# Gate exponentials in PSUM, 32-bit zero products at the start, and a new order table, in a windowed-attention and adapter-mixture kernel

## The chip, the cores and the metric

The kernel runs on one core of a Trainium2 chip. The metric is the device time of one execution in microseconds (us). The kernel before was timed three times: 145.18, 145.84 and 146.81 us, median 145.84. One further execution was taken by the hardware profiler, and every row shown here is from that one.

## The reference

Eight batches of eight heads attend over 576 positions with a window of 32 to each side; the heads of a batch are laid side by side into rows of 512, and each of the 4608 rows goes through a mixture of eight low-rank adapters (rank 16) of which the two with the highest gate logits are used.

```
scores = scale * (q @ k.T);  scores = where(|i - j| <= 32, scores, -1e9)
attn   = softmax(scores);    x = (attn @ v) as (4608, 512)
logits = x @ w_gate;         the two largest, w = softmax over these two
out    = x + sum over the two experts of w * ((x @ A[e]) @ B[e])
```

## The kernel before, in words

*Names.* TensorE (PE) multiplies, VectorE (DVE) and ScalarE (ACT) move results out of PSUM, GpSimd (POOL) casts inputs and issues the loads of v, SyncE (SP) issues the other loads and all stores. PSUM has eight banks, and the program hands them out as buffers of one or two ("B").

*Loads.* q, k and v are each cut into nine tiles (t = 0 to 8). A tile of q or k is one load on SP's queue (L287) into one of five buffers `raw`; two casts (L296 on ACT, L298 on POOL or DVE) turn its halves into 16 bits (`c16`, six buffers); eight transposes on PE for each half (L306) and an eviction (L316) make `qT` and `kT`. A tile of v comes in four loads on POOL's queue (L328), which write 16 bits, and is turned on DVE (L337).

*Attention.* 36 score tiles: two mask products (L392) and 16 to 20 score products (L397) into two PSUM banks, one exponential on ACT (L404) into `PT`. The products with v (L434, 26 matmuls for a head's five row groups) go to two banks `po`; DVE takes the reciprocal of the row sums (L446) and scales (L459) into `xs`.

*Adapters.* Four sets of rows (s = 0 to 3); the first three are handled ten row groups at a time, the last in parts of 4, 4 and 2, so there are six passes. A pass transposes `xs` (L487), multiplies with `A` and the gate weights at once (L523, forty matmuls in the first three passes) into buffers `pz` of two banks, and then runs the gate on DVE: maximum and difference (L534, L535), the exponential on ACT (L542, `gexp`), then `gate2` (L548 to L555), in which L553 compares the exponentials with the second largest, L554 multiplies the result with them and L555 multiplies with the reciprocal of the sum. `gated` (L565) multiplies the adapter's inner values in PSUM with the gates and frees the `pz` banks. Then transposes (L574), an eviction (`zT`), the second product (L602, with L605 adding x on PE in all but the first set), the copy or sum into `ob` (L613, L616) and the store (L623).

*Order.* The program makes a list of operations, each with its engine or engines, its buffers and its needs. The table `ORDER` gives the order in which they are issued, `ON` the engine where there is a choice, and `HOME` the number of the buffer. Each engine then runs its own instructions strictly in that order, with waits for data and for free buffers. An argument `need` between operations without shared data only restricts the table; it puts no wait into the program. At the start 16 matmuls of zeros (`zw`, L220) run on PE before the first data is there.

## Time and profile before

| | us |
|---|---|
| median of three runs | 145.84 (145.18 to 146.81) |
| the profiled execution's own time | 144.93 |
| its span, first to last instruction | 143.2 |
| busy in the span: PE / DVE / ACT / POOL | 113.8 / 95.8 / 85.9 / 51.3 |
[...]

The span is 1.73 us shorter than the execution's time. A busy PE in the profile is not PE at its peak, since matmuls overlap and their ends are modelled. [...] "Idle before" in a row is the time for which the engine stood still in front of that instruction, with the instruction that ended it.

### The profile page before, as it was taken

The numbers are of one execution on the slowest core, as the hardware profiler recorded it, in microseconds if no ns is written. First come the engines' busy times: TensorE is split into PE (matmuls) and PEld (weight loads), VectorE is DVE, ScalarE is ACT, GpSimd is POOL, SyncE is SP. The second block draws the span as 40 slices with busy tenths as digits, with TensorE's granted clock in tenths as the row PEclk, the third lists the DMA queues.
The fourth block names the chain that finished last, engine by engine and source line by source line (L and its number), as shares of the span: only waits on it lengthen the run. The fifth ranks groups of instructions, "written<-read, shape, count | busy, mean of one in ns | idle before, by whom it ended". The sixth has DMA issues, their size and how long they took to land.

```text
span 143.2 us, 5190 instructions
## 1 busy us (share of the span) xinstructions
PE 113.8 (80%) x2246; PEld 84.5 (59%) x2246; DVE 95.8 (67%) x180; ACT 85.9 (60%) x124; POOL 51.3 (36%) x86
## 2 busy tenths in 40 slices
PE   5934769949797986396999808999899999699840
PEld 2324457747694875275878707667689667577410
DVE  2206536895297869955997895687699688748710
ACT  7214196738775958053886820777639676478770
POOL 6983069459435869404308693000000000000000
PEclk9998777999999999959999985799999999999999
DMA  4999999999999999997487997037000523317885
GB/s 124 361 286 266 301 413 363 338 322 378 334 299 410 323 404 356 285 298 307 79 317 150 292 248 150 0 143 280 13 0 5 183 61 131 123 65 292 281 315 181
DMA packets 13223, 33.90 MB, mean 237 GB/s; under 512 B 2704, under 2 KB 2704, under 8 KB 13200
## 3 DMA queue, kind: packets, MB, share of 16 engines
q1 hardware_dynamic: 11472, 28.86, 55.4%
q0 software_dynamic: 1728, 4.72, 18.0%
q8 instruction: 17, 0.28, 0.8%
q14 instruction: 6, 0.05, 0.1%
HBM read 28.85 MB, written 9.44 MB: 267 GB/s over the span
## 4 chain that ended last, share of the span: by engine, by line
PE 64%; DVE 13%; DMA 11%; issue 5%; ACT 2%; SPq 1%; DVEq 0%; ACTq 0%
PE banks L397 13%; DMA raw<-in_q_dram 11%; PE banks L434 11%; PE banks L306 8%; PE banks L392 7%; PE banks L487 6%; PE banks L602 6%; PE banks L523 6%; PE banks L605 4%; DVE sm L553 3%; DVE sm L555 2%; PE banks L574 2%; DVE xs L459 2%; DVE sm L554 2%; DVE zs L565 1%
## 5 line engine op out<-in xcount | busy, mean ns | idle before, releaser
L404 ACT ACTIVATE PT<-banks 128x1024 f16<-128x1024 f32 x36 | 36.2, 1023 | 15.2 <-PE banks L397 11.8
L298 POOL CAST c<-raw 128x1024 f16<-128x1024 f32 x29 | 29.8, 1045 | 27.9 <-DMA raw<-in_k_dram 12.4
L459 DVE TENSOR_TENSOR xs<-banks,rc 128x640 f16<-128x640 f32 (+1 forms) x33 | 26.4, 802 | 2.3 <-PE banks L487 1.3
L306 PE MATMUL banks<-ident,c 128*128 128x128 f16 x288 | 20.6, 230 | 8.6 <-DVE c L298 4.4
L434 PE MATMUL banks<-vt,PT 64*128 64x65 f16 x832 | 18.9, 194 | 7.2 <-DVE zs L565 3.6
L397 PEld LDWEIGHTS <-kT 64*64 64x64 f16 x608 | 18.8, 114 | 9.9 <-issue 9.8
L397 PE MATMUL banks<-qT,kT 64*64 64x128 f16 (+3 forms) x608 | 24.2, 225 | 0.1
L306 PEld LDWEIGHTS <-c 128*128 128x128 f16 x288 | 18.0, 103 | 10.1 <-DVE c L298 4.5
L434 PEld LDWEIGHTS <-PT 64*128 64x128 f16 x832 | 15.2, 96 | 10.5 <-issue 8.7
L328 POOL DMA_DIRECT2D v<-in_v_dram x36 | 17.9, 502 | 7.3 <-DVE vt L337 5.9
L337 DVE STREAM_TRANSPOSE vt<-v 128x1024 f32<-128x1024 f32 x9 | 18.7, 2072 | 0.6 <-DMA v<-in_v_dram 0.6
L392 PE MATMUL banks<-mask,twice 64*128 64x512 f16 x72 | 15.4, 419 | 4.5 <-DVE zs L565 4.2
L613 ACT COPY ob<-banks 128x1024 f32<-128x1024 f32 (+1 forms) x15 | 13.8, 934 | 3.5 <-PE banks L605 3.0
L602 PE MATMUL banks<-Bw,zT 128*128 128x512 f16 x40 | 14.6, 386 | 1.0 <-DVE zT L177 1.0
L446 DVE RECIPROCAL rc<-banks 128x10 f32<-128x10 f32 (+1 forms) x33 | 7.1, 215 | 12.3 <-PE banks L434 9.1
L179 ACT COPY xT<-banks 128x512 f32<-128x512 f32 x16 | 8.9, 592 | 6.2 <-PE banks L487 6.1
L605 PE MATMUL banks<-xs,ident 128*128 128x512 f16 x30 | 11.6, 386 | 0.0
L487 PE MATMUL banks<-ident,xs 128*128 128x128 f16 x160 | 10.8, 220 | 0.9 <-DVE xs L459 0.9
L487 PEld LDWEIGHTS <-xs 128*128 128x128 f16 x160 | 9.7, 115 | 2.1 <-DVE xs L459 1.0
L523 PE MATMUL banks<-WA,xT 128*128 128x136 f16 x160 | 10.8, 223 | 0.2 <-issue 0.2
L316 ACT COPY kT<-banks 128x512 f32<-128x512 f32 x15 | 8.5, 596 | 4.0 <-PE banks L306 4.0
L316 ACT COPY qT<-banks 128x512 f32<-128x512 f32 x13 | 7.5, 595 | 5.5 <-PE banks L306 5.5
(49 smaller groups left out, 102.9 us busy)
## 6 DMA issues: line engine op xcount, KB each, us to landing
raw<-in_k_dram SPq DMA_DIRECT2D x9, 1024.0 KB, 15.6
raw<-in_q_dram SPq DMA_DIRECT2D x9, 1024.0 KB, 14.7
out_dram<-ob SPq DMA_DIRECT2D x24, 256.0 KB, 2.8
v<-in_v_dram POOLq DMA_DIRECT2D x36, 128.0 KB, 6.8
out_dram<-ob SPq DMA_DIRECT2D x16, 192.0 KB, 2.6
ob<-in_moe_A_dram SPq DMA_DIRECT2D x1, 256.0 KB, 19.5
ob<-in_moe_B_dram SPq DMA_DIRECT2D x1, 256.0 KB, 19.6
wgf<-in_moe_w_gate_dram SPq DMA_DIRECT2D x1, 16.0 KB, 8.1
```

The source lines that it names most:

```text
L298: (nc.vector if eng == "DVE" else nc.gpsimd).tensor_copy(out=o, in_=i)
L306: nc.tensor.matmul(out=ap16(tp)[:, 128 * r:128 * r + 128], lhsT=ap(c16)[:, r], rhs=ident, is_transpose=True, start=True, stop=True)
L328: op("POOL", 0.62, lambda p0=p0, f=f, g=g: nc.gpsimd.dma_start(out=ap(v16)[p0:p0 + 32], in_=src[32 * t:32 * t + 32, f, g]), bufs=[v16], ne ...
L337: nc.vector.transpose(out=o, in_=i)
L392: nc.tensor.matmul(out=p[:, 4 * j:4 * j + 4], lhsT=twice[m], rhs=bcast(mask[m], 1, 4), start=True, stop=False)
L397: nc.tensor.matmul(out=p[m, i, c0:c0 + w], lhsT=ap(kT[t])[m, 64 * s:64 * s + 64], rhs=ap(qT[tq])[m, c:c + w], start=False, stop=(n == len( ...
L404: op("ACT", act(1024), lambda: nc.scalar.activation(out=ap(pt)[:, :, 64:192].rearrange("m i (x b r) -> m i x b r", b=2, r=16), in_=ap(ps). ...
L434: nc.tensor.matmul(out=ap(po)[:, 512 * g + VD * j:512 * g + VD * j + VD], lhsT=ap(PT[ti])[m, pos, off:off + 128], rhs=ap(vt[t])[m, sl, 0:V ...
L459: nc.vector.tensor_tensor(out=o, in0=i, in1=ap(rc)[:, 0:n].to_broadcast([128, n, 2, D]), op=ALU.mult)
L487: nc.tensor.matmul(out=ap16(tp)[:, 512 * i + 128 * c:512 * i + 128 * c + 128], lhsT=ap(xs[s])[:, b, g].rearrange("p (m c) -> p c m", c=4)[ ...
L523: nc.tensor.matmul(out=ap(pz)[:, o:o + ER + E], lhsT=ap(xT)[:, i, c, :], rhs=WA[:, c, :], start=(c == 0), stop=(c == 3))
L602: nc.tensor.matmul(out=o, lhsT=ap(zT)[:, j + i], rhs=Bw, start=True, stop=not by_pe)
```

## The change

Four things are changed at once.

1. The exponentials `e` of the gate are no longer kept in SBUF beside the differences `d` but in PSUM, in 80 unused columns behind the results in the first `pz` buffer. So every operation of `gate2` that has two tensors reads at most one from SBUF. L554 and L555 are also changed round: first `e * sv`, written back to PSUM, then that product times the mask.
2. The zeros of the first products are 32 bits instead of 16, and there are 4 products instead of 16.
3. The rule that the first tile of v is issued after the first load of k in the table (`V_AFTER`) is gone.
4. The tables `ORDER`, `ON` and `HOME` are found anew.

```
-    zw = sb.tile([128, 128], F16, name="zw")
+    zw = sb.tile([128, 128], F32, name="zw")
...
-                    bufs=[v16], need=[(V_AFTER, 0, "raw")] if t == 0 else [],
+                    bufs=[v16],
...
         def pieces():
             a = ap(sm)
-            small = [a[:, 10 * i:10 * i + n] for i in range(3)]
-            wide = [a[:, 40 + 80 * i:40 + 80 * i + E * n].rearrange("p (g e) -> p g e", e=E)
-                    for i in range(3)]
-            return small + wide
+            small = [a[:, 10 * i:10 * i + n].rearrange("p (w g) -> p w g", w=nw) for i in range(3)]
+            wide = [a[:, 40 + 80 * i:40 + 80 * i + E * n].rearrange("p (w g e) -> p w g e", w=nw, e=E)
+                    for i in range(2)]
+            e = ap(pzs[0])[:, 4 * GS + ER + E:4 * GS + ER + E + E * n].rearrange(
+                "p (w g e) -> p w g e", w=nw, e=E)
+            return small + wide + [e]
...
-            m1, m2, sv, d, e, g = pieces()
+            m1, m2, sv, d, g, e = pieces()
             nc.scalar.activation(out=e, in_=d, func=AF.Exp)
...
-            nc.vector.tensor_tensor(out=g, in0=e, in1=bcast(m2, 2, E), op=ALU.is_ge)
-            nc.vector.tensor_tensor(out=g, in0=g, in1=e, op=ALU.mult)
-            nc.vector.tensor_tensor(out=g, in0=g, in1=bcast(sv, 2, E), op=ALU.mult)
-        op("DVE", 1.5, gate2, bufs=[sm], need=[("g2", tok)], make=[("g3", tok)], prio=pr + 1)
+            nc.vector.tensor_tensor(out=g, in0=e, in1=bcast(m2, 3, E), op=ALU.is_ge)
+            nc.vector.tensor_tensor(out=e, in0=e, in1=bcast(sv, 3, E), op=ALU.mult)
+            nc.vector.tensor_tensor(out=g, in0=e, in1=g, op=ALU.mult)
+        op("DVE", 1.5, gate2, bufs=[sm, pzs[0]], need=[("g2", tok)], make=[("g3", tok)], prio=pr + 1)
...
-WARM = 16
-V_AFTER = "k"
+WARM = 4
...
 ORDER = (
-    3, 22, 17, 6, 61, 10, 15, 62, 4, 11, 16, 0, 35, 36, 5, 28, 64, 47, 63, 39, 40, 20, 41, 1, 37,
+    0, 3, 35, 8, 63, 28, 22, 19, 10, 64, 44, 17, 4, 9, 5, 45, 39, 47, 18, 7, 6, 42, 62, 36, 12,
```

Three places show what moves. The first is DVE in the gate of the first pass, before; `sm` is the SBUF buffer of the gate, `banks` is PSUM.

```order
L550 TENSOR_REDUCE sm_102<-sm_102 128x10
L551 TENSOR_SCALAR sm_102<-sm_102 128x10
L552 RECIPROCAL sm_102<-sm_102 128x10
L553 TENSOR_TENSOR sm_102<-sm_102 128x80
L554 TENSOR_TENSOR sm_102<-sm_102 128x80
L555 TENSOR_TENSOR sm_102<-sm_102 128x80
L565 TENSOR_TENSOR zs_94<-banks,sm_102 128x640
L565 TENSOR_TENSOR zs_95<-banks,sm_102 128x640
```

The three products of 80 columns read SBUF alone. Now the same place on DVE after the change (the lines are shifted by five).

```order
L553 SCALAR_TENSOR_TENSOR sm_102<-sm_102,banks 128x80
L555 TENSOR_REDUCE sm_102<-sm_102 128x10
L556 TENSOR_SCALAR sm_102<-sm_102 128x10
L557 RECIPROCAL sm_102<-sm_102 128x10
L558 TENSOR_TENSOR sm_102<-banks,sm_102 128x80
L559 TENSOR_TENSOR banks<-banks,sm_102 128x80
L560 TENSOR_TENSOR sm_102<-banks,sm_102 128x80
L570 TENSOR_TENSOR zs_94<-banks,sm_102 128x640
```

The number and size of the instructions stay; each one with two tensors now has `banks` among its inputs, and one writes there.

The second place is SP's queue where the last loads (into `raw`) meet the first stores, before.

```order
L287 DMA raw_65<-in_q_dram 128x2x1024
L287 DMA raw_62<-in_k_dram 128x2x1024
L287 DMA raw_61<-in_q_dram 128x2x1024
L623 DMA out_dram<-ob_99 96x512
L287 DMA raw_64<-in_q_dram 128x2x1024
L623 DMA out_dram<-ob_98 128x512
L623 DMA out_dram<-ob_100 128x512
```

One store stood in front of the last of the 18 loads. The same place on SP after the change:

```order
L288 DMA raw_64<-in_q_dram 128x2x1024
L288 DMA raw_65<-in_k_dram 128x2x1024
L628 DMA out_dram<-ob_100 128x512
L628 DMA out_dram<-ob_99 128x512
L288 DMA raw_61<-in_k_dram 128x2x1024
L628 DMA out_dram<-ob_100 128x512
L628 DMA out_dram<-ob_99 96x512
L288 DMA raw_63<-in_k_dram 128x2x1024
L288 DMA raw_64<-in_q_dram 128x2x1024
L628 DMA out_dram<-ob_99 128x512
```

Two stores now stand in front of the 16th load and two more in front of the 17th and 18th. On PE the first adapter product that leads to a store (L602, now L607) comes after 824 matmuls, where 1095 stood in front of it before; the first L523 (now L529) comes after 602, before after 700. The zero products are among these, 4 now and 16 before, and all matmuls are 2234 instead of 2246.

The third place is POOL at the start, before: the loads of v and the building of the mask.

```order
L328 DMA v_72<-in_v_dram 32x2048 x2
masks.py:197 MEMSET ident 128x128
masks.py:199 ISA
masks.py:199 AFFINE_SELECT ident<-ident 128x128
L328 DMA v_72<-in_v_dram 32x2048 x2
L185 MEMSET mask_110 128x128
L188 AFFINE_SELECT mask_110<-mask_110 64x128
L191 AFFINE_SELECT mask_110<-mask_110 64x128
L188 AFFINE_SELECT mask_110<-mask_110 64x128
L191 AFFINE_SELECT mask_110<-mask_110 64x128
L195 COPY mask<-mask_110 128x128
L328 DMA v_73<-in_v_dram 32x2048 x4
```

After the change POOL has there:

```order
masks.py:197 MEMSET ident 128x128
masks.py:199 ISA
masks.py:199 AFFINE_SELECT ident<-ident 128x128
L329 DMA v_72<-in_v_dram 32x2048 x2
L329 DMA v_73<-in_v_dram 32x2048 x3
L329 DMA v_72<-in_v_dram 32x2048
L329 DMA v_73<-in_v_dram 32x2048
L329 DMA v_72<-in_v_dram 32x2048
L186 MEMSET mask_110 128x128
L189 AFFINE_SELECT mask_110<-mask_110 64x128
L192 AFFINE_SELECT mask_110<-mask_110 64x128
```

Eight loads of v, those of the first two tiles, now stand in front of the mask, where four did; the first five loads on SP are the same as before.

## Rows read from the trace of the kernel before

**Rows 1.** The page: the chain of work that ended last, by engine

```profile
PE 64%; DVE 13%; DMA 11%; issue 5%; ACT 2%; SPq 1%; DVEq 0%; ACTq 0%
```

**Rows 2.** Timeline of PE, first gate: start us, us, engine, line, operation, [idle before]

```profile
55.35 0.63 PE L397 MATMUL banks<-qT,kT 64*64 64x32 f16 x18
59.53 0.58 PE L434 MATMUL banks<-vt,PT 64*128 64x65 f16 x26 [3.55 <-DVE zs L565]
```

**Rows 3.** Timeline of PE, second gate

```profile
86.33 0.61 PE L392 MATMUL banks<-mask,twice 64*128 64x512 f16 x2 [4.24 <-DVE zs L565]
```

**Rows 4.** Timeline of DVE, first gate

```profile
51.65 0.20 DVE L535 TENSOR_TENSOR sm<-banks,sm 128x40 f32<-128x40 f32 x1
...
54.37 2.78 DVE L553 TENSOR_TENSOR sm<-sm 128x80 f32<-128x80 f32 x1
57.19 0.24 DVE L554 TENSOR_TENSOR sm<-sm 128x80 f32<-128x80 f32 x1
57.47 1.15 DVE L555 TENSOR_TENSOR sm<-sm 128x80 f32<-128x80 f32 x1
```

**Rows 5.** Timeline of POOL beside it

```profile
51.61 2.02 POOL L298 CAST c<-raw 128x1024 f16<-128x1024 f32 x2 [1.32 <-DMA raw<-in_q_dram]
...
56.00 1.05 POOL L298 CAST c<-raw 128x1024 f16<-128x1024 f32 x1
...
57.46 1.05 POOL L298 CAST c<-raw 128x1024 f16<-128x1024 f32 x1
```

**Rows 6.** Timeline of DVE, second gate

```profile
80.03 0.98 DVE L553 TENSOR_TENSOR sm<-sm 128x80 f32<-128x80 f32 x1
81.04 2.19 DVE L554 TENSOR_TENSOR sm<-sm 128x80 f32<-128x80 f32 x1
83.27 2.15 DVE L555 TENSOR_TENSOR sm<-sm 128x80 f32<-128x80 f32 x1
```

**Rows 7.** Timeline of POOL beside it

```profile
79.88 1.04 POOL L298 CAST c<-raw 128x1024 f16<-128x1024 f32 x1 [1.75 <-issue]
```

**Rows 8.** Timeline of DVE, third gate, after POOL's last cast

```profile
113.36 0.18 DVE L553 TENSOR_TENSOR sm<-sm 128x80 f32<-128x80 f32 x1
113.58 0.24 DVE L554 TENSOR_TENSOR sm<-sm 128x80 f32<-128x80 f32 x1
113.85 0.24 DVE L555 TENSOR_TENSOR sm<-sm 128x80 f32<-128x80 f32 x1
```

**Rows 9.** Stretches: us, busy us of each engine (instructions), granted clock, DMA share, GB/s

```profile
4.00:8.00 4.00, 4.00 (x24) 1.96 (x23) 0.83 (x2) 1.11 (x2) 3.68 (x11) 1.00 1.06 343
...
10.00:12.50 2.50, 0.00 (x0) 0.00 (x0) 0.65 (x1) 0.66 (x1) 2.04 (x8) 1.00 1.06 264
12.50:15.00 2.50, 2.27 (x18) 1.66 (x19) 2.31 (x5) 1.52 (x4) 0.00 (x0) 0.58 1.04 272
...
59.60:64.30 4.70, 4.70 (x121) 3.41 (x121) 2.92 (x7) 2.05 (x2) 0.00 (x0) 0.64 1.04 289
...
86.30:91.70 5.40, 5.37 (x50) 4.19 (x50) 3.76 (x4) 1.94 (x3) 0.93 (x3) 0.53 0.41 71
```

**Rows 10.** Groups by shape: busy us, mean ns of one, idle before

```profile
L554 DVE TENSOR_TENSOR sm<-sm 128x32 f32<-128x32 f32 x2 | 0.4, 192 | 0.1
...
L565 DVE TENSOR_TENSOR zs<-banks,sm 128x256 f16<-128x256 f32 x1 | 0.4, 423 | 0.0
```

**Rows 11.** Timeline: the 16th load, its cast and transposes, and the first store

```profile
53.66 0.37 SPq L287 DMA_DIRECT2D raw<-in_k_dram  x1
...
66.28 1.04 POOL L298 CAST c<-raw 128x1024 f16<-128x1024 f32 x1 [7.35 <-DMA raw<-in_k_dram]
...
70.63 0.37 SPq L623 DMA_DIRECT2D out_dram<-ob  x1
...
80.38 1.50 PE L306 MATMUL banks<-ident,c 128*128 128x128 f16 x24 [0.18 <-ACT PT L404]
```

**Rows 12.** Timeline of POOL at the start: the last step of the mask

```profile
9.86 2.25 POOL L205 TENSOR_SCALAR_AFFINE_SELECT twice<-twice 64x32 f16<-64x32 f16 x8
```

## The prediction

> **What bounds the kernel now.** I read the chain of waits first. TensorE holds 64% of it, VectorE 13%, the transfers 11% [rows 1]. The 11% is the wait for the first tiles; the reader should be surprised by VectorE's 13%, since this engine does small things beside TensorE. So I asked next where TensorE stands still after the start. Two waits stand out, 3.55 us in front of 59.53 [rows 2] and 4.24 us in front of 86.33 [rows 3], and both end with line 565, the last operation of a gate. It is the operation that frees the PSUM banks `pz`, and TensorE's next products want banks.

> Then the timeline of VectorE in front of each of the two. In the first gate L553 takes 2.78 us and L555 1.15 us, while L554, with as many columns, takes 0.24 [rows 4]. In the second the three take 0.98, 2.19 and 2.15 [rows 6]. In the third they take 0.18, 0.24 and 0.24 [rows 8]. Same instructions, same sizes, and up to fifteen times the duration: this is no work, it is a wait inside an instruction. Beside it I laid the timeline of POOL. L553 of the first gate ends at 54.37 + 2.78 = 57.15, and POOL's cast ends at 56.00 + 1.05 = 57.05; L555 ends at 58.62 and a cast at 58.51 [rows 4, 5]. L553 of the second gate ends at 81.01, a cast at 80.92 [rows 6, 7]. The third gate comes when POOL has cast its last. So an operation on two SBUF tensors waits until POOL's cast is over. And the form that the change goes to is in the trace as well: L535, with one input in PSUM and one in SBUF, runs at 51.65 in the middle of two casts (51.61 to 53.63) and takes 0.20 [rows 4, 5].

> Last, the clock. From 59.60 to 64.30 the granted clock averages 0.64 and from 86.30 to 91.70 0.53, with TensorE busy all the time [rows 9]. Both stretches stand right behind the two waits, and before each the engine did nothing for some 4 us. Half speed is thus a second price of the same wait.

> **The change part by part.** The sum is made against the profiled execution's 144.93 us, 0.9 under the median of 145.84.

> *Exponentials in PSUM.* What goes: in the first gate 2.78 - 0.18 = 2.60 and 1.15 - 0.24 = 0.91, together 3.51 of the 3.55 us for which TensorE stands still. In the second 0.80 + 1.95 + 1.91 = 4.66, more than the 4.24 us of the wait, so all 4.24 go. Together 7.75 us. With the waits gone the reason for half speed goes: 4.70 x (1 - 0.64) = 1.69 and 5.40 x (1 - 0.53) = 2.54, together 4.23 us; TensorE is busy in both stretches, so I take them as bound by its clock.

> What comes: four VectorE operations in each of six gates read `e` from PSUM, one of them writes there, and ScalarE's exponential writes there. No row shows VectorE or ScalarE writing a gate to PSUM. From below: L535 with 40 columns takes 0.20 [rows 4], L554 in SBUF 0.192 for 32 columns [rows 10] and 0.24 for 80 [rows 8], which makes 1 ns a column and 0.20 for 40, so a PSUM input costs nothing; less than nothing has no reason, as the columns stay. From above: L565 with 256 columns takes 0.42 [rows 10], 0.18 over L554; five operations in six gates would give 30 x 0.18 = 5.4 us if all of it were on the path. I take zero, by the nearer row in size and kind.

> [...]

> *What is late next.* TensorE now comes to its transposes earlier, so the loads could take the wait's place. The 16th load, issued at 53.66, is waited for by POOL until 66.28 and cast by 67.32; the transposes that use it begin at 80.38 [rows 11]. Without the first wait and its slow stretch TensorE is there at 80.38 - 3.55 - 1.69 = 75.1, still 7.8 us behind the cast. The loads do not bind there. POOL itself gains nothing: its casts take 1.05 with or without VectorE beside them.

> *32-bit zero products.* They only use the time until the first tiles are there. From 10.00 to 12.50 TensorE does nothing at all, and from 12.50 to 15.00 its clock is at 0.58 although the zero products had it at 1.00 from 4.00 to 8.00 [rows 9]. What they win is lost before it is wanted, so I cost this edit at nothing. It is hidden as long as the four are done by 12.5. Bounds: if they kept the clock up until the second tile, 2.50 x 0.42 = 1.05 us could be won; if they ran over by as much as that idle stretch is long, 2.5 us would be lost. The nearest row is the busy 4.00 to 8.00, which leaves them done before 10, so zero.

> [...]

> *v not held.* The rule puts no wait into the program. What moves is POOL's queue: eight loads of v instead of four stand before the mask. The last step of the mask ended at 9.86 + 2.25 = 12.11 [rows 12], and eight loads (two, two and four) stood in front of that step in the old order as well, so I expect it no later than before, and TensorE does nothing until 12.5 in any case [rows 9]. In the transfers, up to four loads of 0.128 MB come forward; at 343 GB/s [rows 9] that is 1.5 us by which the first k tile can be later. TensorE waits for the q tile behind it, in front of which the same loads stood anyway. Zero, between 0 and 1.5.

> *New order.* This can't be priced instruction by instruction. It keeps the work (2234 matmuls for 2246, the difference being the zero products). From below: the remaining waits of TensorE without a named cause are 5% of 143.2, 7 us [rows 1], and a good order may win a third of it, 2.5. From above: the old order was made for gates without the wait, as the new one is, so I see no reason for a loss beyond some 2 us. I take zero.

> Sum: 144.93 - 7.75 - 4.23 = 132.95, forecast 133.0 us, 131 to 135 with the costs taken as zero a little off.

> **The rivals.** *The order wins as well.* The first gate's products come after 602 instead of 700 matmuls, so more of the adapter work fits into the time in which TensorE waits for tiles. With the 2.5 us above: 130.4. For it speaks that early stretch; against it, that the loads keep their pace whatever the order.

> *The wait is shorter but stays.* A gate is a chain of small operations even undisturbed. If the new order has too little beside it, TensorE stops for some 2 us and the clock falls again. Then the 4.23 us of slow stretches are not won: 137.2. For it speaks that the clock is down in both stretches behind a wait; against it, that in the old order the work beside the gates would have covered all but 0.04 us of them.

> *The loads stand behind stores (slower).* The 16th load now waits in SP's queue for two stores, and behind these stand the 17th and 18th with two more. A store waits for its rows of the first set to be added up. The load took 66.28 - 53.66 = 12.62 us to land and 1.04 to be cast, and TensorE wants it at 75.1; so it must be issued by 61.5, and each us later costs one. The first store was issued at 70.63 before [rows 11]; if it still were, the time would be 133 + 9.1 = 142.1. Slower by over 1% (146.4) needs a first store after 61.5 + 13.4 = 74.9, or a second wait of the same kind; I price that case at 147. Against it: the first product that leads to a store stands after 824 matmuls now, and in the old trace that number was reached in the score products at 55.35 [rows 2].

> *The change does not do what it says.* Then something else than the second SBUF input makes VectorE wait, the three operations stay at 1 to 3 us beside POOL's casts, and the time stays at 145. Against it stands L535 in the midst of two casts.

> **How the numbers follow.** The forecast of 133.0 has 0.55, the better order (130.4) 0.17, the shorter wait (137.2) 0.18, no effect (145) 0.05, the loads behind stores (147) 0.05. The range of 129.5 to 139.0 holds the first three with most of their spread, and the upper bound of the PSUM cost (133.0 + 5.4 = 138.4); what is left out is the last two and some tail, under 2 in 10. About 1% is what a measurement of this kernel can tell from no change. Faster by over 1% are the first three cases: 0.90. Within 1% is the case of no effect, 0.05. Slower is the case of the stores, 0.05.

> **What would show it right or wrong.** In the profile after: the three products of 80 columns (L558 to L560) take 0.18 to 0.30 us in all three large gates, beside POOL's casts; no wait of TensorE over 1 us ends with the line that now is `gated` (L570); the stretches behind the gates have a granted clock near 1.00; VectorE's share in the chain of waits falls well under 13%; the span is near 143.2 - 12.0 = 131.2. If the products are short and the time is still over 137, the step on the clock or on what is late next is wrong: then look for a wait of POOL for transfers, with SP's first store after 61.5. If they stay long, the cause of the wait is wrong. If PSUM operands are dear, the four operations are at 0.3 to 0.4 in the last, small gates too.

## The result and the profile after

The kernel after takes 139.41 us (median of 4 runs, 138.75 to 139.61); the kernel before took 145.76 beside it. The ratio is 0.955, 95% interval [0.948, 0.961]. The forecast was 133.0 with a range of 129.5 to 139.0: the direction is right, the time lies 0.4 us outside the range, and of 12.8 us expected 6.4 came. The profiled execution took 138.75 us with a span of 137.0 and a mean granted TensorE clock of 0.969 of full speed (before 144.93, 143.2 and 0.939). From here on a median is over all timed runs of a kernel, while a ratio leaves out the slow runs on both sides, those more than 1.5% above the kernel's fastest, so the two can differ.

First the chain of waits on the page after, which answers to [rows 1]:

```profile
PE 44%; DMA 35%; issue 6%; DVE 5%; ACT 3%; POOL 2%; SPq 1%; POOLq 0%; ACTq 0%; DVEq 0%
```

VectorE's 13% is down to 5%, so most of what the gates had in the chain is gone. The transfers went from 11% to 35%. The table of waits of TensorE says where:

```profile
PE banks L307 <- POOL c L299: 5.6, 4, 2.5
PE banks L307 <- DVE c L299: 4.0, 2, 3.7
PE banks L435 <- issue: 3.7, 3, 2.5
PE banks L307 <- issue: 1.6, 1, 1.6
...
PE banks L398 <- issue: 1.4, 1, 1.4
PE banks L435 <- DVE zs L570: 0.9, 2, 0.6
```

(Line, what was waited for: us in all, times, longest. L307 are the transposes of a cast tile, L435 the products with v, L398 the scores.) L570 is the last operation of a gate, the L565 of [rows 2, 3]: 7.79 us there are now 0.9. In their place stand 5.6 us for tiles that POOL casts, and "issue", waits without a named cause. Their places in the timeline of PE:

```profile
50.56 0.58 PE L435 MATMUL banks<-vt,PT 64*128 64x65 f16 x26 [0.65 <-DVE zs L570]
...
57.40 1.03 PE L307 MATMUL banks<-ident,c 128*128 128x128 f16 x8 [2.48 <-POOL c L299]
...
71.52 0.27 PE L435 MATMUL banks<-vt,PT 64*128 64x65 f16 x6 [2.46 <-issue]
```

and what POOL waited for in front of 57.40:

```profile
46.77 2.03 POOL L299 CAST c<-raw 128x1024 f16<-128x1024 f32 x2
48.73 1.46 POOL L329 DMA_DIRECT2D v<-in_v_dram  x3
56.30 2.02 POOL L299 CAST c<-raw 128x1024 f16<-128x1024 f32 x2 [6.11 <-DMA raw<-in_q_dram]
```

That is q tile 5, late by a wait of 6.11 us of POOL and 2.48 of TensorE. The first gate in the timeline of DVE, for [rows 4]:

```profile
47.27 0.23 DVE L553 SCALAR_TENSOR_TENSOR sm<-sm,banks 128x80 f32<-128x80 f32 x1
47.53 0.24 DVE L555 TENSOR_REDUCE sm<-sm 128x10 f32<-128x80 f32 x1
47.80 1.04 DVE L556 TENSOR_SCALAR sm<-sm 128x10 f32<-128x10 f32 x1
48.87 0.22 DVE L557 RECIPROCAL sm<-sm 128x10 f32<-128x10 f32 x1
49.00 0.18 DVE L558 TENSOR_TENSOR sm<-banks,sm 128x80 f32<-128x80 f32 x1
49.12 0.25 DVE L559 TENSOR_TENSOR banks<-banks,sm 128x80 f32<-128x80 f32 x1
49.40 0.24 DVE L560 TENSOR_TENSOR sm<-banks,sm 128x80 f32<-128x80 f32 x1
...
83.76 0.48 DVE L556 TENSOR_SCALAR sm<-sm 128x10 f32<-128x10 f32 x1
```

The products are short. But L556, ten columns, took 1.04 us and ended at 48.84, when the cast pair of 46.77 ended (48.80): a new hold, which the second gate shows again (the last row). And the stretches that answer to [rows 9] (us; busy us of PE, its weight loads, DVE, ACT and POOL; granted clock, DMA share, GB/s):

```profile
51.00:56.00 5.00, 3.93 (x95) 2.68 (x87) 2.63 (x6) 3.54 (x6) 0.00 (x0) 1.00 1.06 286
56.50:60.00 3.50, 2.60 (x19) 2.05 (x20) 2.85 (x3) 0.58 (x1) 2.11 (x3) 0.52 1.01 352
71.50:74.50 3.00, 2.98 (x59) 2.17 (x60) 2.57 (x3) 1.53 (x3) 0.00 (x0) 1.00 1.02 421
86.00:92.00 6.00, 4.41 (x142) 3.53 (x143) 3.53 (x7) 3.09 (x6) 0.00 (x0) 1.00 0.40 111
```

Half clock is a reading of 0.50: in quarter-us windows of the two profiles the clock reads 1.00 or 0.50, with a value between only where it changes (after, 0.84 from 56.50 to 56.75, 0.50 from there to 60.00, and 0.84 again to 60.25). Behind both gates (51 to 56 and 86 to 92 us) the clock is full, at 1.00. The half clock is now behind the late tile: 3.5 x 0.48 = 1.7 us. Behind the "issue" wait of 2.46 us at 71.52, just as long as the tile's 2.48, it stayed full.

The 6.2 us by which the span shrank, from the two profiles: waits for gates 7.79 to 0.92, -6.9; time lost to half clock over the span (8.7 = 143.2 x 0.061, to 4.2 = 137.0 x 0.031), -4.5; waits for casts of later tiles (1.9 to 5.6), +3.7; waits "issue" (5.5 to 7.0), +1.5; from TensorE's last product to the end (5.2 to 6.6), +1.4. This makes -4.8; smaller waits and a first tile 0.5 us earlier are the rest. The term of the clock is an estimate, and not all of it belongs to the gates. From 10 to 25 us, ahead of every gate, the granted clock was 0.77 before and 0.89 after, which is 1.8 us of the 4.5; and the four runs of the kernel after had mean clocks from 0.923 to 0.969 with times within 0.9 us of each other, so the clock differs from run to run and half clock is not always time lost.

### The profile page after: what moved, and what is told of

Its sections match the earlier page's. It is cut to its first block, busy times and chain, and to the rows that moved or that the text cites. A ratio compares the mean times of both kernels' runs of the same rounds, so it can differ in the third digit from the quotient of the medians.

```text
span 137.0 us, 5167 instructions
## 1 busy us (share of the span) xinstructions
PE 110.1 (80%) x2238; PEld 82.2 (60%) x2238; DVE 90.3 (66%) x182; ACT 85.3 (62%) x124; POOL 49.9 (36%) x84
## 4 chain that ended last, share of the span: by engine, by line
PE 44%; DMA 35%; issue 6%; DVE 5%; ACT 3%; POOL 2%; SPq 1%; POOLq 0%; ACTq 0%; DVEq 0%
DMA raw<-in_k_dram 19%; DMA raw<-in_q_dram 14%; PE banks L435 9%; PE banks L398 8%; PE banks L307 6%; PE banks L488 5%; PE banks L529 5%; PE banks L607 4%; PE banks L393 4%; PE banks L610 3%; DMA out_dram<-ob 3%; POOL c L299 2%; ACT ob L618 1%; DVE xs L460 1%; PE banks L579 1%
## 5 line engine op out<-in xcount | busy, mean ns | idle before, releaser
L405 ACT ACTIVATE PT<-banks 128x1024 f16<-128x1024 f32 x36 | 36.2, 1024 | 12.4 <-PE banks L398 11.6
L299 POOL CAST c<-raw 128x1024 f16<-128x1024 f32 x27 | 27.5, 1046 | 33.1 <-DMA raw<-in_k_dram 14.6
L307 PE MATMUL banks<-ident,c 128*128 128x128 f16 x288 | 22.1, 230 | 11.1 <-POOL c L299 5.6
L307 PEld LDWEIGHTS <-c 128*128 128x128 f16 x288 | 18.3, 103 | 14.9 <-POOL c L299 6.8
L398 PE MATMUL banks<-qT,kT 64*64 64x128 f16 (+3 forms) x608 | 22.8, 216 | 1.7 <-issue 1.4
L398 PEld LDWEIGHTS <-kT 64*64 64x64 f16 x608 | 17.4, 108 | 10.3 <-issue 9.9
L435 PE MATMUL banks<-vt,PT 64*128 64x65 f16 x832 | 17.5, 190 | 4.6 <-issue 3.7
L435 PEld LDWEIGHTS <-PT 64*128 64x128 f16 x832 | 14.5, 94 | 7.2 <-issue 5.3
L618 ACT COPY ob<-banks 128x1024 f32<-128x1024 f32 (+1 forms) x14 | 12.5, 928 | 5.3 <-PE banks L610 3.7
L607 PE MATMUL banks<-Bw,zT 128*128 128x512 f16 x40 | 14.9, 393 | 0.4 <-ACT zT L180 0.4
L393 PE MATMUL banks<-mask,twice 64*128 64x512 f16 x72 | 14.1, 386 | 0.6 <-ACT PT L405 0.4
L297 ACT CAST c<-raw 128x1024 f16<-128x1024 f32 x6 | 6.3, 1050 | 9.9 <-DMA raw<-in_q_dram 9.9
L529 PE MATMUL banks<-WA,xT 128*128 128x136 f16 x160 | 10.8, 223 | 0.3 <-issue 0.3
L529 PEld LDWEIGHTS <-xT 128*128 128x128 f16 x160 | 9.8, 98 | 1.3 <-issue 0.5
```

Source lines behind the costliest of these rows:

```text
L299: (nc.vector if eng == "DVE" else nc.gpsimd).tensor_copy(out=o, in_=i)
L307: nc.tensor.matmul(out=ap16(tp)[:, 128 * r:128 * r + 128], lhsT=ap(c16)[:, r], rhs=ident, is_transpose=True, start=True, stop=True)
L393: nc.tensor.matmul(out=p[:, 4 * j:4 * j + 4], lhsT=twice[m], rhs=bcast(mask[m], 1, 4), start=True, stop=False)
L398: nc.tensor.matmul(out=p[m, i, c0:c0 + w], lhsT=ap(kT[t])[m, 64 * s:64 * s + 64], rhs=ap(qT[tq])[m, c:c + w], start=False, stop=(n == len( ...
L405: op("ACT", act(1024), lambda: nc.scalar.activation(out=ap(pt)[:, :, 64:192].rearrange("m i (x b r) -> m i x b r", b=2, r=16), in_=ap(ps). ...
L435: nc.tensor.matmul(out=ap(po)[:, 512 * g + VD * j:512 * g + VD * j + VD], lhsT=ap(PT[ti])[m, pos, off:off + 128], rhs=ap(vt[t])[m, sl, 0:V ...
```

## The experiments

Each kernel ran with several timed rounds. "Kernel after" in an edit is the changed kernel. The kernel before had medians of 144.5 to 145.8 us on the chips used, and the kernel after came to 0.955, 0.953 and 0.968 of it on three of them, so what is compared closely ran on one chip.

**One part alone.** e1 is the kernel before with only the PSUM edit (its order and its zero products):

```
-            wide = ... for i in range(3)]            # d, e, g in SBUF
+            e = ap(pzs[0])[:, 4 * GS + ER + E:4 * GS + ER + E + E * n]...
```

> The kernel before with the exponentials in PSUM alone: its own order, sixteen 16-bit zero products. Theory T (the gates' waits go as forecast, and TensorE then runs into tiles and instruction blocks that the transfers bring late): the three products of a gate take 0.18 to 0.30 us, no wait over 1 us ends with a gate, and the time is 137 to 141 us all the same, with new waits for POOL's casts. Rival O (the new order is what loses the rest, and the forecast's sum holds for the old one): 132 to 134 us, without such waits. If the products stay long beside POOL's casts, both fall: 145.

Measured: 139.26 us (137.31 to 140.91) against 145.04. Both theories miss: the time is T's, but TensorE has no new wait for POOL's casts. No wait ends with a gate any more, though the second gate's three products run beside a cast (0.18, 0.25 and 0.24 us). Its profile (137.31 us):

```profile
62.89 0.78 PE L435 MATMUL banks<-vt,PT 64*128 64x65 f16 x39 [2.30 <-issue]
...
86.54 0.58 PE L435 MATMUL banks<-vt,PT 64*128 64x65 f16 x26 [1.43 <-ACT ob L618]
```

```profile
64.00:68.00 4.00, 4.00 (x66) 3.50 (x61) 2.40 (x6) 2.27 (x4) 1.29 (x2) 0.57 0.89 343
```

Against the forecast's 133.0 there are 4.3 us too many, and three places in this profile add up to as much: the "issue" wait of 1.16 us at 66.33 before is 2.30, at the same instruction, +1.1; half clock comes back behind it, 4.0 x 0.43 = 1.7; an output buffer that waits for a store holds TensorE for 1.43. So in the old order the tiles are indeed not late, and other waits take the gain.

e2 is the reverse, all but the PSUM edit:

```
-    exponentials in PSUM
+    exponentials in SBUF; ORDER, ON, HOME and the 32-bit zeros of the kernel after
```

> The kernel after with the exponentials back in SBUF: the new order, 32-bit zeros, v not held. Theory T: in the new order the first two gates stand beside POOL's casts too, so some of the three products take 1 to 3 us again and TensorE waits 3 to 8 us for them; part of that is hidden behind the transfers, which are late anyway: 142 to 147 us. Rival O (the new order loses 6 us by itself): 150 us or more. If the order was made so that the gates miss the casts: 139 to 140, with products at 0.18 to 0.25.

Measured: 139.88 us (138.10 to 141.42); ratio 0.970 [0.952, 0.989], beside 0.965 [0.946, 0.983] of e1. The third expectation comes nearest: in the new order only L548, the first product, is held, for 1.57 us at 46.45 and 0.77 at 83.97.

```profile
46.45 1.57 DVE L548 SCALAR_TENSOR_TENSOR sm<-sm 128x80 f32<-128x80 f32 x1
...
45.88 2.03 POOL L298 CAST c<-raw 128x1024 f16<-128x1024 f32 x2
```

The other products of these gates come when POOL casts nothing, since it issues loads or waits itself. Each half of the change alone brings what both bring, as far as these intervals tell.

e4 has sixteen 16-bit zero products (`F16`, `WARM = 16`) in place of four 32-bit ones:

> The kernel after with sixteen 16-bit zero products in place of four 32-bit ones, nothing else. Theory T: same busy time of the zero products (5.7 to 5.8 us) and the same total, 139.4 within 0.7 us; TensorE's stream is a few instructions longer, so the waits that come every 256 instructions fall at another place of the program by as many instructions, which may move the time by up to 1 us either way. Rival Z (32-bit zeros cost what is missing): 1.5 to 5 us faster.

Measured: 139.13 us (137.04 to 140.77). No difference that can be told (ratio 0.965 [0.948, 0.982]). The products are busy for 5.87 us as sixteen and 5.69 as four of 32 bits (5.20 to 6.21 in other profiles of four), so here one of 32 bits took about as long as four of 16, 1.42 and 0.37 us each.

**Are the transfers late?** e5 leaves out most of v:

```
-                    out=ap(v16)[p0:p0 + 32], in_=src[32 * t:32 * t + 32, f, g]),
+                    out=ap(v16)[p0:p0 + 32] if t < 3 else ap(v16)[p0:p0 + 32, 0:1],
+                    in_=src[32 * t:32 * t + 32, f, g] if t < 3 else src[32 * t:32 * t + 32, f, g, 0:1]),
```

> The kernel after, but of the v tiles 3 to 8 only one column of 1024 is loaded (24 transfers of 0.128 MB become almost nothing), so 3 MB of some 18 MB are left out and those blocks of the output are not computed from v. Theory T (transfers late): the waits of TensorE for POOL's casts (1.20, 1.52 and 2.48 us at 17.86, 29.36 and 57.40) and the waits every 256 instructions shrink to a third or less, and the time is 131 to 135 us. Rival O (the order, or the gates themselves, hold the rest): 138 to 140 us, with the waits of TensorE elsewhere.

Measured: 132.83 us (129.81 to 134.37), ratio 0.915 [0.893, 0.937], clear of the kernel after. The stretch of 50 to 60 us is full and at full clock:

```profile
50.00:60.00 10.00, 10.00 (x239) 7.54 (x233) 9.05 (x12) 8.35 (x14) 6.78 (x9) 1.00 0.46 114
```

The waits for POOL's casts fell from 5.6 to 2.0. The "issue" waits only fell from 7.0 to 5.1, where T had said a third or less. So bytes that move ahead of 57 us make the tiles late.

e10 left out 2 MB at the other end, most of the last two tiles:

```
+        out=ap(raw) if t < 8 else ap(raw)[:, 0:1, 0:64],
+        in_=src if t < 8 else src[:, 0:1, 0:64]),
```

> The kernel after, but of the last two tiles (q 8 and k 8, the 17th and 18th load, issued at 63.68 and 64.18) only 64 columns of the first half are loaded, so 2 MB less moves between 64 and 72 us and those blocks of the output are not computed from the inputs. Theory F (the waits without a named cause are instruction blocks that stand behind data in the transfers): the wait of 2.46 us at 71.52 falls below 1 us, the earlier ones stay (0.97 at 23.94, 1.43 at 37.15), the time falls by 1 to 3 us. Rival P (the wait belongs to that place of the program, whatever moves): 2.3 to 2.7 us there again, and less than 0.7 us gained.

Measured: 139.35 us, ratio 0.964 [0.959, 0.969], against 139.11 and 0.953 [0.946, 0.960] of the kernel after on its chip (a0 below). 2 MB less late in the program bring nothing. Of the "issue" wait it says nothing: 2.72 us at 72.84, but the stretch of 64 to 72 us was as full as in a0 (248 and 250 GB/s), though 2 MB were left out.

**Which transfer?** e6 moves the 16th load ahead of the stores, which tests the prediction's slower rival:

```
-  ... store, store, load k 7, store, store, load k 8 ...
+  ... load k 7, store, store, store, store, load k 8 ...
```

> The kernel after with one line of its order moved: the 16th load (a k tile) is issued ahead of the four stores of the first output rows instead of behind two of them. Its buffer was free at about 49 us, it was issued at 61.59. Theory T (what is late is what TensorE waits for at 17.86, 29 and 57.40, all of it ahead of this load): 139.4 within 0.7 us, because TensorE waits for nothing that this load brings; POOL's wait of 8.22 us to 74.84 gets shorter and buys nothing. Rival S (the loads behind the stores, a rival of the prediction, are what is late): 1.5 to 4 us faster.

Measured: 138.17 us (136.17 to 139.30), ratio 0.962 [0.941, 0.982]: no gain that can be told. POOL's wait of 8.22 us for the load is gone (it now waits 6.2 us for TensorE, which is to free the buffers of casts). In the kernel after the first store went out at 60.65 and the 16th load at 61.59, as late as the prediction feared, but TensorE was late too.

e7 issues five quarters of v tiles 5 and 6 behind the casts of q tile 5; e8 exchanges the loads of q 5 and q 7 with their buffers; e9 does both:

```
e7   v quarters 158, 156, 157, 137, 140: now behind operation 124 (cast of q 5)
e8   ORDER: 161 <-> 123 (loads of q 7 and q 5); HOME: their buffers, and that of k 8
```

> The kernel after with five quarters of the v tiles 5 and 6 issued behind POOL's casts of the q tile that TensorE waits for at 57.40, instead of ahead of them; the same bytes in all. 5 x 0.131 MB at some 340 GB/s are 1.9 us. Theory T (transfers ahead of 57 us are the bound): that q tile is cast about 1.5 to 2 us earlier, the wait of 2.48 us falls below 1, and the time is 0.7 to 3 us lower. Rival L (the time won at 57 us is lost again behind it, to later loads or instruction blocks): the wait falls, and the time is the same within 0.5 us.

> The kernel after with two loads exchanged: the q tile that TensorE waits for at 57.40 (tile 5) is issued where the later one (tile 7) was, into its buffer, and tile 7 where tile 5 was. The bytes are the same, one tile of 1 MB fewer stands ahead of the late one: 1.05 MB at 340 GB/s are 3.1 us. Theory T: no wait over 0.5 us at 57, no half-clock stretch behind it (2.6 us busy at 0.58), 2 to 4 us faster. Rival L (the next tile is as late): the wait moves to tile 6 behind it, less than 1 us faster.

> Both: the five v quarters behind the casts and the two q loads exchanged. Theory T: 2.5 to 5 us faster than the kernel after, the stretch of 50 to 60 us busy for over 9 us. Rival L: no better than the better one of the two alone, and under 1 us in all.

Measured, on a chip where the kernel after did not run: 138.59, 138.24 and 137.83 us, ratios 0.971 [0.962, 0.981], 0.968 [0.958, 0.978], 0.960 [0.949, 0.971]. The mechanism of T is there, its size is not. In e7 the wait of 2.48 us at 57 is 0.31 (at 56.01). In e8 it is gone, and the next ones are longer:

```profile
61.88 1.07 PE L307 MATMUL banks<-ident,c 128*128 128x128 f16 x16 [1.58 <-POOL c L299]
...
70.79 0.30 PE L435 MATMUL banks<-vt,PT 64*128 64x65 f16 x6 [3.19 <-issue]
```

```profile
70.00:75.00 5.00, 4.21 (x55) 2.86 (x56) 3.00 (x3) 1.31 (x2) 0.48 (x1) 0.66 1.00 406
```

This is Rival L: what is won at 57 us is mostly lost by 71, and half clock follows the longer wait. Next, e9 and the kernel after (a0) on one chip:

> The kernel after, unchanged, beside the next three on one chip, to know what its time is there and how far its waits vary between two profiles. Every theory: 0.955 of the kernel before within 0.01; the waits without a named cause at the same instructions as in its first profile.

> The kernel with the five late v quarters and the two q loads exchanged, once more, on the same chip as the kernel after. Theory T in its first form (transfers ahead of 57 us alone): 2.5 us under the kernel after. Theory T2 (the time won at 57 us comes back as a longer wait for an instruction block near the 1089th matmul, as its first profile showed with 4.35 us): 0 to 1.5 us under it, that wait again over 3 us.

Measured: a0 139.11 us (137.68 to 142.31), ratio 0.953 [0.946, 0.960]; e9 137.12 (136.11 to 138.47), ratio 0.949 [0.943, 0.955]. By the ratios this is 0.5 us less, which can't be told from nothing; the "issue" wait is 2.87 us at 68.87. T in its first form (2.5 us) is out, and T2 fits in time, though the wait is a little under the 3 us it gave.

**What are the "issue" waits?** Position first. In the kernel after and the kernels made from its order there is a wait of 2.4 us or more at one place, behind 1,119 recorded matmuls, at times from 65.6 (e5) to 74.1 us (e4), in the middle of one operation of 26 matmuls (L435) whose data are all there. The place is one of the instruction stream and not of the work: e4 has eight recorded matmuls more at its start, and its wait, again behind 1,119, stands eight products earlier in the work, behind 38 of a row of 52 and not behind 46:

```profile
74.09 0.51 PE L435 MATMUL banks<-vt,PT 64*128 64x65 f16 x14 [3.08 <-issue]
```

In the 18 profiles of this case there are 84 "issue" waits over 0.2 us, and each stands behind 95 matmuls and a multiple of 128. A matmul has its weight load, so 128 are 256 recorded instructions. Then the queue "instruction" in the transfers (packets, MB, share of 16 engines), in narrow windows of the kernel after, here 69.0 to 69.5 us:

```profile
q8 instruction: 1, 0.02, 11.0%
```

The page lists 17 such packets with 0.28 MB, 16 KB each, for 4,476 recorded instructions of TensorE, 263 to a packet. Such a packet starts 2.2 to 2.7 us before the end of every one of the 84 waits: the end at 71.52 has its packet at 69.28, that at 37.15 at 34.75, that at 90.11 at 87.77. From this spacing and these packets the author's reading is that TensorE is out of instructions and waits for its next block, here called an instruction block. e11 adds traffic where there is little:

```
+    for i in range(10):
+        extra = buf("raw", f"extra{i}")
+        op("POOL", 0.62, lambda extra=extra: nc.gpsimd.dma_start(out=ap(extra), in_=run_view("q")[0:128]),
+           bufs=[extra], make=[("extra", i)])
```

> The kernel after with ten needless loads of 1 MB each (a q tile into the five free load buffers, twice) put on POOL's queue behind its last cast, which nobody reads and no one waits for: they keep the transfers full from about 84 to 114 us, where the kernel after has them mostly idle. Theory F (instruction blocks stand behind data): new waits of TensorE without a named cause, 0.5 to 3 us each and some 128 matmuls or a multiple apart, between 90 and 115 us, where the kernel after has one of 1.59 at 90.11 and none behind it; the time rises by 3 to 8 us. Rival P (those waits belong to their places in the program): none between 95 and 115 us; the time rises by under 1 us, or by waits that end with a store.

Measured: 145.39 us, ratio to before 1.000 [0.994, 1.006], by the ratios 6.8 us over the kernel after (a0).

```profile
109.97 0.39 PE L393 MATMUL banks<-mask,twice 64*128 64x512 f16 x2 [2.08 <-DVE ob L618]
...
118.87 1.01 PE L435 MATMUL banks<-vt,PT 64*128 64x65 f16 x53 [1.32 <-issue]
```

One new "issue" wait of 1.32 us, where the kernel after has none, and 2.08 us for a store that comes late. The time is what F said, the number of waits is not: between 92 and 117 us, with the transfers full from 100 on (DMA share 1.02 to 1.04), there is none. Both theories hold in part: traffic adds to the wait, and the place decides too. The packets show the first: the block wanted behind 2,015 matmuls has its packet 107 matmuls ahead in the kernel after and 22 ahead in e11. What makes the place behind 1,119 the worst is open. There the packet starts only when TensorE has come to the end of its block, 0.2 us later in the kernel after, and no run shows why it does not start earlier.

**Is the gate free now?** e12 writes the sum of L556 to PSUM:

```
-            nc.vector.tensor_scalar(out=sv, in0=m2, scalar1=1.0, scalar2=None, op0=ALU.add)
-            nc.vector.reciprocal(out=sv, in_=sv)
+            one = ap(pzs[0])[:, 968:968 + n].rearrange("p (w g) -> p w g", w=nw)
+            nc.vector.tensor_scalar(out=one, in0=m2, scalar1=1.0, scalar2=None, op0=ALU.add)
+            nc.vector.reciprocal(out=sv, in_=one)
```

e13 is e12 and e9 together. They ran beside the kernel after (a0 again) and e1:

> The kernel after, unchanged, as the measure for the three beside it on one chip: 0.953 to 0.957 of the kernel before, L556 held for 0.3 to 1.1 us in the first two gates.

> The kernel after with one more piece of the gate in PSUM: the sum m2 + 1 (L556, 128x10) is written to PSUM and the reciprocal reads it there, so that no operation behind the exponential has all its data in SBUF but the maximum L555. Theory H (an operation from SBUF to SBUF with a single input can be held by POOL's cast too, which cost 1.04 us at 47.80 and 0.48 at 83.76): L556 takes 0.17 to 0.25 us in all gates, TensorE's waits for the gates (0.65 and 0.27 us) go, and the time is 0 to 1 us lower. Rival C (the hold belongs to the place in time, any operation issued there is held): L556 or the operation behind it takes 0.4 to 1 us again.

> The five late v quarters, the two q loads exchanged, and the sum in PSUM, together. Theory T2 with H: 1.5 to 3 us under the kernel after, no tile wait of TensorE over 1.5 us behind 20 us, the wait for an instruction block near the 1089th matmul still 2.4 us or more. If the loads were not what is late: less than 1 us under it.

> The kernel before with the exponentials in PSUM alone, once more, on the same chip as the kernel after. Theory Q (in the old order the gain is eaten by other waits than in the new one: the instruction block at 62.89 with half clock behind it, and a store that holds an output buffer): within 1 us of the kernel after, with these waits and without a new tile wait. Rival O (the new order loses): 1.5 us or more under the kernel after.

Measured on one chip, before at 145.60 us: a0 139.68 (137.99 to 140.71), e12 140.40 (137.94 to 142.60), e13 136.85 (135.49 to 138.25), e1 139.13 (137.98 to 142.03). The first gate of e12 (line numbers from L557 on are one higher there), with POOL beside it:

```profile
47.53 0.17 DVE L557 TENSOR_SCALAR banks<-sm 128x10 f32<-128x10 f32 x1
47.74 0.22 DVE L558 RECIPROCAL sm<-banks 128x10 f32<-128x10 f32 x1
47.88 0.18 DVE L559 TENSOR_TENSOR sm<-banks,sm 128x80 f32<-128x80 f32 x1
47.99 0.25 DVE L560 TENSOR_TENSOR banks<-banks,sm 128x80 f32<-128x80 f32 x1
48.28 0.24 DVE L561 TENSOR_TENSOR sm<-banks,sm 128x80 f32<-128x80 f32 x1
```

```profile
46.81 2.04 POOL L299 CAST c<-raw 128x1024 f16<-128x1024 f32 x2
```

The whole gate runs inside a cast pair without a hold: H is shown for L556, and with it what the change claims. No wait of TensorE ends with a gate any more. In the profiles of the new order L556 with its output in SBUF was held eleven times, for 0.36 to 1.39 us, and each time it ended 0.03 to 0.04 us after a cast. The maximum L555 also has one input and its output in SBUF, and it took 0.24 us beside the cast (at 47.53, with a cast from 46.77 to 47.83), so not every such operation is held. The time of e12 is not lower; in its profile the wait for the tile grew:

```profile
57.33 1.03 PE L307 MATMUL banks<-ident,c 128*128 128x128 f16 x8 [3.38 <-POOL c L299]
```

In e5 the first gate stood between two casts and the same operation took 0.17 us with its output in SBUF: whether it is hit is a matter of a microsecond or two. e13 has no tile wait over 1.5 us behind the first tile and 3.15 us "issue" at 69.19; its ratio to before is 0.955 [0.946, 0.964], that of a0 on the same chip 0.968 [0.958, 0.979]. By the ratios e13 is 1.9 us faster, with intervals that overlap a little. Its median is the lowest of a version that does all the work, but the 0.949 of e9 on another chip is not worse. e1, at a ratio of 0.971 [0.963, 0.980], ends with the kernel after, with "issue" 2.01 at 63.17 and no new tile wait (Q); of the store wait only the first e1 tells.

## Why the prediction was wrong

*Exponentials in PSUM.* Right: 7.75 us of waits were to go, 6.9 went. The products are short beside casts (e12). In the old order all of it went (e1). The 0.9 that stayed comes with L556 (1.04 and 0.48 us), which was counted as undisturbed: it takes 0.17 where no cast is beside it. The prediction's own reason, two inputs from SBUF, was too narrow, since L556 has one. Why L556 is held and the maximum L555 is not, no run here shows.

*PSUM operands at no cost.* Right: L559 and L560 take 0.25 and 0.24 with an input in PSUM, where L554 and L555 took 0.24 from SBUF [rows 8].

*The clock.* Right for the gates, both stretches are at 1.00. But the prediction let half clock vanish with its cause and did not ask whether another wait would bring it back: 1.7 us behind the late tile at 57.40, and 1.7 in e1 behind the block at 62.89. The length of a wait does not settle this. Behind 2.30 us in e1 the clock fell; behind 2.46 at 71.52 after (71.5 to 74.5 us), 2.72 in e10 (72 to 80) and 2.87 in the second e9 (60 to 70) it stayed at 1.00. That the mean clock of the whole span rose by as much as the sum wanted (4.5 us for 4.23) is luck, since 1.8 of it lie ahead of the gates.

*What is late next.* This step failed. "The loads do not bind there" was read off one load, the 16th, and it held for that one (e6) and for the two behind it (e10). In the new order other loads are late: q tile 5, which is cast at 56.30, and tiles near 17 and 29 us, 5.6 us of TensorE's waits, shown by e5. Even in the old order, on which that step's arithmetic rests, the sum did not come true (e1), because two more waits were never asked for: the instruction block and the output buffer. The prediction knew the waits without a named cause, but only as 7 us of which an order could win a third, and not as something that could grow; the "issue" row, 1.16 us at 66.33, was there to be read. That a gate's wait had covered the rest of the two is argued, not tried. In the sum this step stood at nothing; it measured 3.7 us of waits for tiles and 1.5 us for blocks, and the 1.7 us of half clock behind the tile.

*New order at zero.* As a number nearly right: e1 on one chip ends where the kernel after does. As a reason wrong, so the number is luck: the order takes the gates away from the casts (e2) and makes the tiles late instead. It also costs about 1 us or more at the end, which the prediction did not look at: from TensorE's last product to the end it is 5.2 us in the three profiles of the old order and 6.0 to 7.0 in the fifteen of the new.

*32-bit zeros and v not held.* Zero each, as said. For the zeros the prediction went by a row of 16-bit products, and no row of the kernel before has a 32-bit one; measured are 5.69 us busy for four of 32 bits (after) and 5.87 for sixteen of 16 (e4), with no difference in time that can be told. The first tile's products began at 12.18 us after, 12.71 before (12.1 to 13.1 in the profiles of the new order). v by itself was not tried.

*The rivals.* "The loads stand behind stores" is out by e6. "The wait is shorter but stays", at 137.2, is nearest in time, but by luck: TensorE still stops for 2 to 3 us and the clock falls once behind such a wait (0.52 from 56.50 to 60.00), though for a tile and an instruction block and not for a gate.

## What to carry to other kernels

A wait that is removed can be paid back by the next resource in line, and this next one must be looked for on every resource, not on the load that one suspects: here tiles, instruction blocks, an output buffer and the clock, each worth 1 to 4 us. Two edits that cure the same wait (operands in PSUM, an order that keeps gates off the casts) did not add up here (ratios 0.965 and 0.970 alone, 0.953 to 0.968 together). And an operation that is short in a trace shows nothing about a contention that it did not meet there.
